# P times V in eight 64x32 array tiles over two PSUM banks: a sliding-window attention block with a gated feed-forward on one Trainium2 core

## The chip, the cores and the metric

The kernel runs on one core of one Trainium2 chip. The metric is device time in microseconds for one execution; the profiled execution is one such run with the hardware profiler on.

## What is computed

x is 2048 x 640. Its normalised form feeds two branches, whose sum is added to x: an attention of 32 heads of 20 dimensions with a causal window of 256, and a gated feed-forward (640 to 1728 and back).

```python
mask = (idx[:, None] - idx[None, :] >= 0) & (idx[:, None] - idx[None, :] < W)   # W = 256
p = softmax(where(mask, q @ k.T * Dh ** -0.5, -1e9))
o = p @ v                       # per head, 2048 x 20
out = x + (o as 2048 x 640) @ wo + (gelu(xn @ w_gate) * (xn @ w_up)) @ w_down
```

## The kernel before

**Stages.** First the layer norm, its transposes and the first projections (until about 100 us); then the attention (about 100 to 570 us); then the rest of the feed-forward; last the down projections. All order on TensorE, ScalarE, VectorE and GpSimd in the attention is the order of the code in `attention` (from L805): nothing is moved by a scheduler.

**Units and slots.** Attention work comes in 32 units, u = 4g + c: eight groups g of eight, each of four heads, and four chunks c of 512 queries. A chunk c > 0 also sees keys of the chunk ahead; a first chunk (c = 0, every fourth unit) does not. Each unit has 14 slots. `SCORES` (L33) says which of the unit's twelve score pieces are made in which slot. `BURSTS` (L32) puts maxima in slots 0, 4 and 8. After every slot's attention work `pull_fill` adds about 2.4 projection matmuls (f32r, 512 columns), so that TensorE always has something to stream.

**Maxima.** `max_pair` (L503) computes q times k for 32-query strips, in eight array tiles of 64 rows by 32 columns: two heads (row halves, each with a PSUM bank of its own) by four strips. VectorE reduces each bank to row maxima (L527). They belong to units one or two ahead. `max_end` (L541) transposes the negated maxima of the next unit in slot 6 (bank `ps_n`), and ScalarE stores them as extra rows of q (L547), so that the scores come out with the maximum already subtracted.

**Scores.** `exp_piece` (L568) makes one score piece for one head: keys on the 128 partitions, queries along the free axis, then ScalarE's exponential (L584) from PSUM into a P tile, f32. The pieces (`pieces`, L549) are packed into three P tiles per unit, X, Z and Y, of four heads each: a key block kb of 128 keys meets the 384 queries from its own start on, cut to the chunk. GpSimd sets what lies outside the window to zero one slot after a tile's last head (`clear`, L588, with L595 for the diagonal and L598 for the far edge). There are three P buffers.

**P times V.** `av_unit` (L601), in slot 0 of the next unit, multiplies the P tiles with v (21 columns per head, the last of ones for the softmax sum; 32 are loaded). Each head has a column tile of the array, 128 rows by 32 columns at `(0, 32 * j)`; all key blocks accumulate in one bank `ps_o`, 24 matmuls for c > 0, 16 for a first chunk. ScalarE copies the bank to `ob` (L613), and three slots later SyncE stores it (L617, L618).

**The ring.** The banks of the maxima, the scores, the negated maxima and P times V all come from one ring of six PSUM banks, tag `ring` (L482, L498); a matmul that takes a bank waits until its former tenant has been read (VectorE for `ps_m`, ScalarE for `ps_e`, `ps_o`, `ps_n`). Which bank is handed out is decided when the program is built. In slot 0 the order is: two pairs of maxima (four banks), P times V (one), two pairs of maxima (four), one score.

**GpSimd** also makes the low parts of split operands (L259, L643) and sums of x (L740), which fill its free time.

Of the kernel before, what the change touches and what calls it, by code (L numbers as in the profile page):

```python
# [9 lines left out]
F32 = mybir.dt.float32  # L10
F32R = mybir.dt.float32r
BF = mybir.dt.bfloat16
AF = mybir.ActivationFunctionType
OP = mybir.AluOpType
# [5 lines left out]
C = 512  # L20
# [9 lines left out]
QROWS = 64 + SR  # L30
NS = 14
BURSTS = 0, 4, 8  # L32
SCORES = {0: range(0, 1), 2: range(1, 5), 4: range(5, 7), 8: range(7, 9), 10: range(9, 12)}  # L33
RATE = 34.05
V1_AT = "gu", 0, 3
VEARLY = 2
# [34 lines left out]
def block_kernel(ctx, tc, x, wqk, wv, wgu, wdo, wdl, out):  # L71
    nc = tc.nc
# [120 lines left out]
    done = set()  # L193
    now = [None]

    def at(slot, fn, *a):
        acts.setdefault(slot, []).append((fn, a))
# [31 lines left out]
    def defer(n, fn, *a):  # L229
        if now[0] is None:  # L230
            fn(*a)
        else:
            at(now[0] + n, fn, *a)
# [190 lines left out]
    with tc.tile_pool(name="lp", bufs=1, side="right") as lp:  # L424
# [5 lines left out]
        ps = psd.tile([128, C], F32, name="ps_u", tag="dn")  # L430
# [49 lines left out]
    vtiles = dict(enumerate(v0[2]))  # L480
    pf.close()
    psr = pp.enter_context(tc.tile_pool(name="psr", bufs=6, space=PSUM, reuse_waits="tile"))  # L482
    ap = pr.enter_context(tc.tile_pool(name="ap", bufs=2, side="right", reuse_waits="tile"))
# [14 lines left out]
    def bank(name):  # L498
        return psr.tile([128, C], F32, name=name, tag="ring")
# [49 lines left out]
    def pieces(c):  # L549
        b = 4 * c  # L550
        X = [(b, 0, 0, 384)] + ([(b - 2, 384, 0, 128)] if c else [])
        Y = [(b + 1, 0, 128, 384), (b + 3, 384, 384, 128)]
        Z = ([(b - 1, 0, 0, 256)] if c else []) + [(b + 2, 256, 256, 256)]
        return X, Z, Y
# [11 lines left out]
    pts = {}  # L566
# [21 lines left out]
    def clear(u, bi):  # L588
        c = u % NC
        pt = pts[u, bi]  # L590
        for p in pieces(c)[bi]:
            for col, diag in diag_tail(*p, c):
# [4 lines left out]
                else:  # L597
                    nc.gpsimd.affine_select(out=a, in_=a, pattern=[[0, 4], [-1, 128]], compare_op=OP.is_ge,  # L598
                                            fill=0.0, base=-1, channel_multiplier=1)

    def av_unit(u):  # L601
        g, c = divmod(u, NC)
        o, v = bank("ps_o"), vtiles[g]
        todo = [(pts[u, bi], *p) for bi, ps in enumerate(pieces(c)) for p in ps]
        for i, (pt, kb, col, q0, n) in enumerate(todo):
            assert (id(v), kb) in done, (u, kb)
            for j in range(4):
                w0_ = kb * 84 + 21 * j
                nc.tensor.matmul(o[32 * j:32 * j + 32, q0:q0 + n], v[:, w0_:w0_ + 32], pt[:, j, col:col + n],  # L609
                                 start=i == 0, stop=i == len(todo) - 1, skip_group_check=True,  # L610
                                 tile_position=(0, 32 * j))
        ob = ap.tile([128, C], F32, name="ob", tag="ob", bufs=1)
        nc.scalar.activation(ob, o, AF.Copy)  # L613

        def store():
            for j in range(4):
                nc.sync.dma_start(od[c].rearrange("(d h) t -> h d t", h=H)[4 * g + j], ob[32 * j:32 * j + DH, :])  # L617
            nc.sync.dma_start(sd[c][4 * g:4 * g + 4, :], ob[DH::32, :])  # L618

        defer(3, store)  # L620

    def load_gu(f):
        raws = []
# [163 lines left out]
    def pull_max(n, slot):  # L787
        for _ in range(n):
            x = next(stream, None)
            if x is None:  # L790
                return
            max_pair(*x)
            if x[1] == 7:
                at(slot + (MXD if slot >= 0 else 4), max_end, x[0])
# [10 lines left out]
    def attention():  # L805
# [18 lines left out]
        for u in range(NU + 1):  # L824
            for i in range(NS):
# [5 lines left out]
                if i == 0 and u:  # L831
                    av_unit(u - 1)
                    flush()
                    pull_max(2, T)
                for s in SCORES.get(i, ()) if u < NU else ():
                    exp_piece(u, s)
# [502 lines left out]
    for j, f in enumerate(range(NFA, NF - 1)):  # L1339
        end = f + 1 == NF - 1  # L1340
        first, second = {i: [] for i in range(4)}, {i: [] for i in range(4)}
# [91 lines left out]
    for n, (p, k) in enumerate(steps):  # L1433
        i = n % (NQD + 1)
        if i == 0:
            begun.clear()
            ps = {b: psn.tile([128, C], F32, name=f"ps_{b}", tag=f"b{b}") for b in (1, 2, 5, 3, 6, 4, 7, 8)}
# [71 lines left out]
```

## Time and profile before

| | us |
|---|---|
| median of 3 runs | 1046.93 (1046.66 to 1049.24) |
| the profiled execution | 1046.71 |
| its span, first to last instruction | 1045.0 |
| TensorE busy in the span | 1034.0 |
| P times V, matmul records x1408, busy | 84.9 |
| maxima on VectorE (L527), 512 reductions, busy | 227.9 |
| exponentials on ScalarE (L584), busy | 195.6 |
| copies of P times V (L613), 32, busy | 19.1 |

How to read it: a matmul's busy time overlaps that of its neighbours, since matmuls are pipelined, so start-to-start distances are used for what a block takes. A group's row has its busy time and the mean duration in ns, then the idle time of the engine just ahead of it and who ended that. A timeline row has the start, the duration of the merged run, engine, line, operation, `out<-in`, and in brackets the idle time ahead and its releaser. In windows rows the busy figures stand in the order PE, PEld, DVE, ACT, POOL.

### The profile page before, as it was taken

To read this page: it belongs to the slowest core of one execution; us is meant where nothing else is said; L and a number is where in the kernel's file an instruction comes from. 1 tells how busy PE (TensorE), PEld (TensorE's weight loads), DVE (VectorE), ACT (ScalarE), POOL (GpSimd) and SP (SyncE) were. 2 spreads that over 40 slices of the span, in tenths; PEclk is the share of its full clock that TensorE was granted. 3 is DMA by queue.
4 is the path that set the end of the run, shared out by engine and by line. 5 is a ranking of instruction groups with operands and counts; after the bars stand their busy time and mean duration, and the time that the engine had idled before them with its cause. 6 is when DMAs were issued, how large, how long until landed. Compare 5 with 4: busy or idle time off the path is not lost.

```text
span 1045.0 us, 25814 instructions
## 1 busy us (share of the span) xinstructions
PE 1034.0 (99%) x9533; PEld 826.2 (79%) x9533; DVE 717.1 (69%) x2007; ACT 513.6 (49%) x1088; POOL 335.9 (32%) x511
## 2 busy tenths in 40 slices
PE   8999999999999999999999999999999999999998
PEld 8987666666677766666667888888888999999998
DVE  8745656666655556666663678877656888888887
ACT  4444666765665666555656522223324553333332
POOL 5222767766464458464634111110110000000000
PEclk9999999999999999999999999999999999999999
DMA  5552465545332355444322556677217864443342
GB/s 200 189 150 61 136 185 157 174 152 183 98 117 74 106 148 153 129 131 140 103 80 82 191 193 235 220 254 246 100 61 255 272 232 137 136 128 114 124 136 92
DMA packets 105192, 158.76 MB, mean 152 GB/s; under 512 B 15421, under 2 KB 60093, under 8 KB 105065
## 3 DMA queue, kind: packets, MB, share of 16 engines
q1 hardware_dynamic: 102680, 150.95, 45.1%
q10 hardware_dynamic: 2384, 6.16, 1.8%
q8 instruction: 75, 1.23, 0.5%
q14 instruction: 53, 0.43, 0.1%
HBM read 101.78 MB, written 54.92 MB: 150 GB/s over the span
## 4 chain that ended last, share of the span: by engine, by line
PE 89%; DVE 3%; DMA 3%; POOL 2%; SPq 1%; ACT 1%; issue 1%; DVEq 0%; POOLq 0%
PE ps_g L953 21%; PE ps L1220 21%; PE ps_d L110 19%; PE ps_e L582 7%; PE ps_v L110 7%; PE ps_o L609 7%; PE ps_m L523 4%; PE ps_g L110 1%; DMA qs<-qd 1%; SPq L494 1%; PE ps_t L181 1%; DMA qd<-pt 1%; POOL pt L259 1%; PE ps_d L356 1%; POOL wql L643 0%
## 5 line engine op out<-in xcount | busy, mean ns | idle before, releaser
L527 DVE CUSTOM_DVE_ANT_0 junk<-ps_m,mask 128x288 bf16<-128x288 f32 (+2 forms) x512 | 227.9, 445 | 155.0 <-PE ps_m L523 97.2
L584 ACT ACTIVATE P<-ps_e 128x512 f32<-128x512 f32 (+2 forms) x384 | 195.6, 578 | 59.8 <-PE ps_e L582 56.1
L1220 PE MATMUL ps<-wb,at 128*128 128x320 f32 x999 | 155.9, 309 | 0.0
L1220 PEld LDWEIGHTS ps<-wb,at 128*128 128x128 f32 x999 | 148.9, 188 | 0.2
L595 POOL TENSOR_SCALAR_AFFINE_SELECT P<-P 128x512 f32<-128x512 f32 x128 | 84.6, 663 | 139.1 <-ACT P L584 138.1
L582 PE MATMUL ps_e<-qs,ks 124*128 124x128 bf16 (+2 forms) x704 | 107.4, 277 | 0.6 <-DVE mx L527 0.5
L110 PE MATMUL ps_d<-xh,wqh 128*128 128x512 f32 x350 | 104.3, 410 | 0.0
L110 PE MATMUL ps_d<-xl,wqh 128*128 128x512 f32 x350 | 104.3, 409 | 0.0
L110 PE MATMUL ps_d<-xh,wql 128*128 128x512 f32 x350 | 103.9, 409 | 0.0
L1220 PE MATMUL ps<-wt,at 128*128 128x320 f32 x552 | 89.3, 309 | 0.4 <-DVE u L1058 0.4
L582 PEld LDWEIGHTS <-ks 124*128 124x128 bf16 x704 | 50.9, 98 | 46.5 <-issue 29.0
L609 PE MATMUL ps_o<-P,v 128*32 128x384 f32 (+2 forms) x1408 | 84.9, 386 | 0.7 <-POOL P L598 0.7
L1220 PEld LDWEIGHTS ps<-wt,at 128*128 128x128 f32 x552 | 82.9, 188 | 0.9 <-DVE u L1058 0.9
L598 POOL TENSOR_SCALAR_AFFINE_SELECT P<-P 128x512 f32<-128x512 f32 x112 | 70.3, 638 | 33.6 <-ACT P L584 33.6
L1174 ACT ACTIVATE at<-ss 128x512 fp32r<-128x512 f32 x59 | 37.3, 632 | 87.6 <-DVE ss L1058 87.5
L103 POOL TENSOR_TENSOR wql<-wr,wqh 128x640 fp32r<-128x640 f32 x11 | 17.6, 1607 | 174.8 <-PE ps_g L953 149.5
L609 PEld LDWEIGHTS ps_o<-P,v 128*32 128x32 f32 x1408 | 41.0, 109 | 40.5 <-issue 20.4
L110 PEld LDWEIGHTS ps_d<-xh,wql 128*128 128x128 f32 x350 | 63.9, 189 | 11.1 <-issue 0.4
L110 PEld LDWEIGHTS ps_d<-xl,wqh 128*128 128x128 f32 x350 | 63.8, 189 | 10.4 <-issue 0.2
L110 PEld LDWEIGHTS ps_d<-xh,wqh 128*128 128x128 f32 x350 | 63.5, 189 | 10.7 <-issue 0.2
L259 POOL TENSOR_TENSOR pt<-r,pt 128x512 bf16<-128x512 f32 x40 | 46.8, 1169 | 63.2 <-ACT pt L258 63.0
L613 ACT ACTIVATE ob<-ps_o 128x512 f32<-128x512 f32 x32 | 19.1, 598 | 86.3 <-PE ps_o L609 76.1
(194 smaller groups left out, 1846.8 us busy)
## 6 DMA issues: line engine op xcount, KB each, us to landing
hr<-hd SPq DMA_DIRECT2D x104, 128.0 KB
hd<-he SPq DMA_DIRECT2D x50, 256.0 KB
wr<-wgu SPq DMA_DIRECT2D x27, 320.0 KB
qs<-qd SPq DMA_DIRECT2D x64, 120.0 KB
ks<-kd SPq DMA_DIRECT2D x64, 120.0 KB
xi<-x SPq DMA_DIRECT2D x16, 320.0 KB
qs<-qd SPq DMA_DIRECT2D x64, 80.0 KB
ks<-kd SPq DMA_DIRECT2D x64, 80.0 KB
```

The source lines that it names most:

```text
L110: nc.tensor.matmul(ps, a(k), b(k), start=n == 0, stop=n == 3 * nk - 1)
L259: nc.gpsimd.tensor_tensor(out=pt[:, l, :], in0=r, in1=pt[:, 1, :], op=OP.subtract)
L523: nc.tensor.matmul(ps[32 * h:32 * h + 32, lo:hi], q[rows, j, q0:q0 + 32], keys, start=True, stop=True, tile_position=(64 * r, 32 * h))
L527: nc.vector.tensor_tensor_reduce(out=junk[:, 0:n], in0=ps[:, 0:n], in1=mask[:, 288 - n:288], scale=1.0, scalar=NEG, op0=OP.add, op1=OP.max ...
L582: nc.tensor.matmul(ps[:, col:col + n], k[0:QROWS, j, kc:kc + 128], q[0:QROWS, j, q0:q0 + n], start=True, stop=True)
L584: nc.scalar.activation(pt[:, j, lo:hi], ps[:, lo:hi], AF.Exp, scale=SCALE)
L595: nc.gpsimd.affine_select(out=a, in_=a, pattern=[[0, 4], [1, 128]], compare_op=OP.is_ge, fill=0.0, base=0, channel_multiplier=-1)
L598: nc.gpsimd.affine_select(out=a, in_=a, pattern=[[0, 4], [-1, 128]], compare_op=OP.is_ge, fill=0.0, base=-1, channel_multiplier=1)
L609: nc.tensor.matmul(o[32 * j:32 * j + 32, q0:q0 + n], v[:, w0_:w0_ + 32], pt[:, j, col:col + n], start=i == 0, stop=i == len(todo) - 1, ski ...
L953: nc.tensor.matmul(ps, i, j, start=first and n == 0, stop=n == len(work) - 1, skip_group_check=True)
L1174: nc.scalar.activation(hi[:, 3:7], s, AF.Copy)
L1220: nc.tensor.matmul(ps[bank][:, 0:HD], *work[bank][j], start=bank not in begun, stop=final[p, bank] == n and j == len(work[bank]) - 1, skip ...
```

## The change

P times V runs in eight array tiles of 64 rows by 32 columns: each key block is cut into two halves of 64 keys, a half for each row half of the array, and each half accumulates in a bank of its own. A half of 64 keys meets only 320 queries, not 384; `windows` works out the columns and pairs a half of one block with a half of the same or another, so that two halves run together. ScalarE copies the two banks, the first to `ob`, the second into the third P tile, which has been read by then; GpSimd adds them one slot later, and the store goes one slot later still. `SCORES` has no score in slot 0 any more, three in slot 2 and two in slot 6, where the negated maxima are.

```diff
-SCORES = {0: range(0, 1), 2: range(1, 5), 4: range(5, 7), 8: range(7, 9), 10: range(9, 12)}
+SCORES = {2: range(0, 3), 4: range(3, 5), 6: range(5, 7), 8: range(7, 9), 10: range(9, 12)}
...
+    def windows(c):
+        r = {}
+        for bi, ps in enumerate(pieces(c)):
+            for kb, col, q0, n in ps:
+                for h in range(2):
+                    first = 128 * (kb - 4 * c) + 64 * h
+                    lo = max(0, first) if kb else 0
+                    hi = min(C, first + 320)
+                    r[h, kb - 4 * c] = bi, kb, col + lo - q0, lo, hi - lo
+        pairs = [(0, 0), (-2, -2), (2, -1), (-1, 2), (1, 1), (3, 3)] if c else [(d, d) for d in range(4)]
+        return [[(h, *r[h, d]) for h, d in enumerate(p)] for p in pairs]
+
     def av_unit(u):
         g, c = divmod(u, NC)
-        o, v = bank("ps_o"), vtiles[g]
-        todo = [(pts[u, bi], *p) for bi, ps in enumerate(pieces(c)) for p in ps]
-        for i, (pt, kb, col, q0, n) in enumerate(todo):
-            assert (id(v), kb) in done, (u, kb)
+        halves, v = [bank("ps_o") for _ in range(2)], vtiles[g]
+        todo = windows(c)
+        for i, pair in enumerate(todo):
             for j in range(4):
-                w0_ = kb * 84 + 21 * j
-                nc.tensor.matmul(o[32 * j:32 * j + 32, q0:q0 + n], v[:, w0_:w0_ + 32], pt[:, j, col:col + n],
-                                 start=i == 0, stop=i == len(todo) - 1, skip_group_check=True,
-                                 tile_position=(0, 32 * j))
-        ob = ap.tile([128, C], F32, name="ob", tag="ob", bufs=1)
-        nc.scalar.activation(ob, o, AF.Copy)
+                for h, bi, kb, col, q0, n in pair:
+                    assert (id(v), kb) in done, (u, kb)
+                    rows, w0_ = slice(64 * h, 64 * h + 64), kb * 84 + 21 * j
+                    nc.tensor.matmul(halves[h][32 * j:32 * j + 32, q0:q0 + n], v[rows, w0_:w0_ + 32],
+                                     pts[u, bi][rows, j, col:col + n], start=i == 0, stop=i == len(todo) - 1,
+                                     skip_group_check=True, tile_position=(64 * h, 32 * j))
+        ob, other = ap.tile([128, C], F32, name="ob", tag="ob", bufs=1), pts[u, 2][:, 0, :]
+        nc.scalar.activation(ob, halves[0], AF.Copy)
+        nc.scalar.activation(other, halves[1], AF.Copy)
+        defer(1, lambda: nc.gpsimd.tensor_tensor(out=ob, in0=ob, in1=other, op=OP.add))
...
-        defer(3, store)
+        defer(4, store)
```

On TensorE, around one P times V of a unit with c > 0, the order before (`ps_m` are maxima, `ps_o` is P times V, its inputs a P tile and v):

```order
L523 MATMUL ps_m<-ks_170,qs_168 32x256
L609 MATMUL ps_o<-P,v 32x384 x4
L609 MATMUL ps_o<-P,v 32x128 x4
L609 MATMUL ps_o<-P,v 32x256 x8
L609 MATMUL ps_o<-P,v 32x384 x4
L609 MATMUL ps_o<-P,v 32x128 x4
L523 LDWEIGHTS qs_168
```

And now, in unit 7, with the engines that a matmul waits for (`Activation` is ScalarE, `Pool` GpSimd, `DVE` VectorE):

```order
L523 MATMUL ps_m<-ks_170,qs_166 32x256
L622 MATMUL ps_o<-P,v 32x320 [waits Activation_49,Pool_49]
L622 MATMUL ps_o<-P,v 32x320 [waits DVE_49]
L622 MATMUL ps_o<-P,v 32x320 x6
L622 MATMUL ps_o<-P,v 32x64 [waits Pool_49]
L622 MATMUL ps_o<-P,v 32x128
```

Eight matmuls stand where four stood, each shorter, and the second, which is the first of the upper half, waits for the second bank. In units 0, 4, 7, 10, 11, 20, 25, 26 and 27 that wait is for VectorE, in the others for ScalarE.

On ScalarE, where one copy and the first scores stood before:

```order
L258 ACTIVATE pt<-r 128x512
L613 ACTIVATE ob<-ps_o 128x512
L584 ACTIVATE P<-ps_e 128x512 x7
L656 ACTIVATE gs<-ps_d 128x512
L657 ACTIVATE he<-ps_d 128x512
```

there are now two copies, and at the same place of the program:

```order
L258 ACTIVATE pt<-r 128x512
L626 ACTIVATE ob<-ps_o 128x512
L627 ACTIVATE P<-ps_o 128x512
L584 ACTIVATE P<-ps_e 128x512 x5
L671 ACTIVATE gs<-ps_d 128x512
L672 ACTIVATE he<-ps_d 128x512
```

The second copy writes into a P tile; seven exponentials ahead of the next other work have become five, the two others standing behind the negated maxima.

## The prediction

> **What bounds the kernel now.** I read the page's busy times first, then its chain, then TensorE's waits in the attention stage, then the timelines around one P times V.
>
> ```profile
> span 1045.0 us, 25814 instructions
> PE 1034.0 (99%) x9533; PEld 826.2 (79%) x9533; DVE 717.1 (69%) x2007; ACT 513.6 (49%) x1088; POOL 335.9 (32%) x511
> PE 89%; DVE 3%; DMA 3%; POOL 2%; SPq 1%; ACT 1%; issue 1%; DVEq 0%; POOLq 0%
> ```
>
> TensorE is busy for 99% of the span and is 89% of the chain that ended last. Its waits within 100 to 570 us, where the attention runs, are these:
>
> ```profile
> PE ps_m L523 <- DMA qs<-qd: 1.5, 3, 0.7
> PE ps_m L523 <- ACT ob L613: 0.7, 2, 0.4
> PE ps_o L609 <- POOL P L598: 0.7, 2, 0.5
> PE ps_e L582 <- DVE mx L527: 0.5, 2, 0.3
> ```
>
> So 3.4 us of waiting in 470 us: a microsecond taken from TensorE's stream comes off the time, unless the shorter stream runs into a wait that it does not meet now. Both sides have to be counted, unit by unit.
>
> **P times V itself.** The TensorE timeline of unit 15 (a unit with a predecessor chunk, 24 of the 32 are such):
>
> ```profile
> 329.47 0.45 PE L523 MATMUL ps_m<-ks,qs 60*32 60x32 bf16 x32
> 329.86 2.80 PE L609 MATMUL ps_o<-P,v 128*32 128x384 f32 x48
> 332.58 0.44 PE L523 MATMUL ps_m<-ks,qs 60*32 60x288 bf16 x16
> 332.95 0.34 PE L582 MATMUL ps_e<-qs,ks 124*128 124x384 bf16 x1
> ```
>
> 24 matmuls leave 48 records: each f32 matmul is two passes. Start to start the block takes 332.58 - 329.86 = 2.72 us. The weight loads show the rhythm of the passes:
>
> ```profile
> 330.20 0.13 PEld L609 LDWEIGHTS ps_o<-P,v 128*32 128x32 f32 x4 [0.19 <-POOL P L598]
> 330.53 1.21 PEld L609 LDWEIGHTS ps_o<-P,v 128*32 128x32 f32 x28 [0.19 <-issue]
> 331.93 0.13 PEld L609 LDWEIGHTS ps_o<-P,v 128*32 128x32 f32 x4 [0.19 <-issue]
> 332.25 0.13 PEld L609 LDWEIGHTS ps_o<-P,v 128*32 128x32 f32 x4 [0.19 <-issue]
> ```
>
> Four loads start together each time, one per head, so the four column tiles run side by side. From 330.53 to 331.93 stand seven passes (two of 128 columns, four of 256, one of 384: 1664 columns) in 1.40 us, 0.841 ns a column. One head's 1536 columns, twice, are 2.58 us; 0.14 us of the 2.72 is start and drain. The same rate gives the short block of unit 16 (first chunk, four pieces, 2 x 1152 columns, 1.94 + 0.14 = 2.08):
>
> ```profile
> 344.32 2.15 PE L609 MATMUL ps_o<-P,v 128*32 128x384 f32 x32
> 346.40 0.44 PE L523 MATMUL ps_m<-ks,qs 60*32 60x288 bf16 x16
> ```
>
> **What the change makes of the block.** A half of 64 keys meets at most 320 queries instead of 384. The eight tiles stand in pairs, and a pair lasts as long as its longer half: 320+128+256+192+320+128 = 1344 columns, twice, 2.26 us; first chunk 384+320+256+128 = 1088, 1.83 us. Add 0.02 for the start. If the halves drift freely the bound is each half's own sum, 1280 (2.15 us); if nothing of the shorter windows is gained, 2.58. I take the pairs.
>
> That eight tiles of 64 rows run side by side is shown by the maxima, which already use that shape: in the row at 332.58 sixteen matmuls of 288 columns in bf16 take 0.37 us. One bf16 column is half an f32 one, 0.42 ns, so two rounds of eight are 0.24 us; sixteen in turn would be 1.9 us. For f32 no row shows it; the other end is a rival below.
>
> The 0.13 to 0.15 us that is left, both in that row and ahead of P times V (329.47 to 329.86: 2 x 288 columns are 0.24 of 0.39), is time in which nothing streams, at each passage between tile shapes. After the change the block has the maxima's shape on both sides. I take 0.11 us as gone at each side; nothing gone is the lower bound. The Trainium skill, TensorEngine Tiling (Array Packing), Key Properties, says that "Changing tiling mode (not just tile) drains the TensorE"; the 0.13 to 0.15 us here agree. By that rule both drains go; if the cost were one of a change of data type, neither would, and my sum would give 3 us less.
>
> TensorE's own saving is then 2.72 - 2.28 + 0.22 = 0.66 us in a normal unit and 2.08 - 1.85 + 0.22 = 0.45 us in a first chunk: 24 x 0.66 + 8 x 0.45 = 19 us. Most of it will not arrive, because of the next three terms.
>
> **First term against it: the ring of six banks and VectorE.** Slot 0 takes four banks for maxima, one for P times V, four more for maxima, and a score; afterwards four, two, four. So the last of the eight maxima takes the bank of the fourth of this same slot, and cannot start until VectorE has reduced that one. Before, it took the third's.
>
> ```profile
> 329.87 0.46 DVE L527 CUSTOM_DVE_ANT_0 junk<-ps_m,mask 128x288 bf16<-128x288 f32 x1 [2.53 <-PE ps_m L523]
> 330.48 0.46 DVE L527 CUSTOM_DVE_ANT_0 junk<-ps_m,mask 128x288 bf16<-128x288 f32 x1
> ...
> 331.70 0.46 DVE L527 CUSTOM_DVE_ANT_0 junk<-ps_m,mask 128x288 bf16<-128x288 f32 x1
> 332.08 0.08 DVE L527 DVE_READ_ACCUMULATOR2_ANT mx<- 128x1 f32 x1
> 332.96 0.46 DVE L527 CUSTOM_DVE_ANT_0 junk<-ps_m,mask 128x288 bf16<-128x288 f32 x1 [0.80 <-PE ps_m L523]
> ```
>
> Counted from the first maximum (329.47), VectorE frees the first bank at 0.86, the second at 1.47, the fourth at 2.69; with 0.05 to wake TensorE (from the copy's end at 243.34 to the row at 243.39, below), 2.74. TensorE is ready for the last pair at 0.39 - 0.11 + 2.28 + 0.13 = 2.69 in a normal unit, 2.26 in a first chunk. Before, the last pair started at 0.39 + 2.72 + 0.13 = 3.24, and 2.60 in a first chunk, with VectorE long done. Hence a normal unit gains 3.24 - 2.74 = **0.50 us**, and a first chunk **loses 0.14 us**. The drains and the free drift now hardly matter in these units: VectorE ends the slot.
>
> The order with its waits shows more: in nine units (0, 4, 7, 10, 11, 20, 25, 26, 27) the second bank of P times V is the bank of this slot's *first* maximum, so the block's second matmul waits until 0.91 instead of starting at 0.28. The block ends 0.6 us later: six normal units gain nothing (0.91 + 2.28 + 0.13 = 3.32 against 3.24), the three first chunks lose 0.1 to 0.3.
>
> In two units the last pair waits now for the bank that P times V itself has just filled:
>
> ```profile
> 137.07 0.31 PE L523 MATMUL ps_m<-ks,qs 60*32 60x288 bf16 x7 [0.37 <-ACT ob L613]
> ...
> 242.61 0.42 PE L523 MATMUL ps_m<-ks,qs 60*32 60x288 bf16 x9
> 243.39 0.31 PE L523 MATMUL ps_m<-ks,qs 60*32 60x288 bf16 x7 [0.37 <-ACT ob L613]
> ...
> 242.74 0.60 ACT L613 ACTIVATE ob<-ps_o 128x512 f32<-128x512 f32 x1 [1.36 <-PE ps_o L609]
> ```
>
> Units 2 and 9 lose that wait: in the new order these pairs take maxima's banks. Unit 9's first maximum stands at 239.50, so its last pair starts 3.89 us on; afterwards VectorE, which had other work first (fourth bank free at 242.91), allows 3.46: 0.4 gained. Unit 2 gains 0.9, with some waiting for GpSimd taken off. Two more kinds of unit differ:
>
> ```profile
> 314.60 0.38 PE L523 MATMUL ps_m<-ks,qs 60*32 60x32 bf16 x28
> ...
> 316.40 0.42 DVE L527 CUSTOM_DVE_ANT_0 junk<-ps_m,mask 128x256 bf16<-128x256 f32 x1
> ...
> 179.85 0.69 DVE L273 TENSOR_TENSOR r<-ps_d,pt 128x512 f32<-128x512 f32 x1 [1.53 <-ACT pt L277]
> ...
> 182.28 0.46 DVE L527 CUSTOM_DVE_ANT_0 junk<-ps_m,mask 128x288 bf16<-128x288 f32 x1
> ```
>
> In units 6, 14, 18 and 22 (here 14) the first four maxima are those of a first chunk and shorter, VectorE is done 2.2 us after the first, and TensorE's 0.31 - 0.11 + 2.28 + 0.13 = 2.61 decides against 3.16 before: 0.55 each, a little less in unit 22. In unit 5 VectorE begins with other work and frees the fourth bank 182.74 - 179.48 = 3.26 us after the first maximum: no gain there.
>
> Sum: nine plain normal units x 0.50 = 4.5; units 6, 14, 18 and 22, 2.1; units 30 and 31, with no maxima around the block, 2 x 0.44 = 0.9; units 2 and 9, 1.3; unit 5, -0.1; the six normal units of the nine, -0.1; first chunks, five x -0.14 and three together -0.7, -1.4. That is **7.2 us**.
>
> **Second term: GpSimd.** It gets one add of 128x512 per unit, which also waits for ScalarE's second copy.
>
> ```profile
> L740 POOL TENSOR_TENSOR tx<-tx,xl 128x256 f32<-128x256 f32 x48 | 35.6, 742 | 1.7
> L103 POOL TENSOR_TENSOR wql<-wr,wqh 128x640 fp32r<-128x640 f32 x11 | 17.6, 1607 | 174.8 <-PE ps_g L953 149.5
> 329.96 0.63 POOL L595 TENSOR_SCALAR_AFFINE_SELECT P<-P 128x512 f32<-128x512 f32 x1
> 336.02 0.63 POOL L595 TENSOR_SCALAR_AFFINE_SELECT P<-P 128x512 f32<-128x512 f32 x1 [3.92 <-ACT P L584]
> ```
>
> Between 742 ns for 256 columns and 1607 for 640 I take 1.3 us. It stands ahead of the clears of the next P tiles. In unit 15 it falls into an idle time of 3.92 us. The last clear of that unit ends at 330.59, 0.73 us after the block has started, and the new block first needs it some 1.9 us after that start: over 1 us to spare. But some units are full:
>
> ```profile
> 179.90:194.90 15.00, 15.00 (x203) 9.76 (x195) 9.71 (x37) 9.63 (x19) 14.30 (x23) 1.00 0.57 171
> sum 462.60, PE 458.82 PEld 306.17 DVE 277.34 ACT 288.79 POOL 273.04; mean PE 14.80 PEld 9.88 DVE 8.95 ACT 9.32 POOL 8.81
> ```
>
> Here GpSimd (the fifth figure after the length) has 0.70 us free, where the mean unit has 6.1. In about three such units the add makes the last clear late by up to 0.5 us: 1.2 us in all, from 0 to 4.
>
> **Third term: ScalarE and DMA.** The second copy costs ScalarE what the first does:
>
> ```profile
> 332.72 0.60 ACT L613 ACTIVATE ob<-ps_o 128x512 f32<-128x512 f32 x1 [2.66 <-PE ps_o L609]
> ```
>
> Both copies end 0.14 + 1.2 = 1.34 us after the block. The scores of slot 2, which take those two banks, come after the last pair (0.13), its drain and two slots of projection work (1.1 us), at about 1.4 us, and the second bank goes to the third of them. It fits, and the score no longer in slot 0 gives ScalarE its 0.6 back there. Slot 6 now has two exponentials behind the negated maxima; slot 8's scores need their banks some 2 us later, where ScalarE takes 0.3 + 1.2. I put 0.5 us on collisions, and 0.5 us on the early waits for qs (the 1.5 us above), which a shorter stream reaches sooner. The store moves one slot behind the add; SyncE's next loads are five slots on.
>
> **Sum.** 7.2 - 1.2 - 0.5 - 0.5 = 5.0 us off. The profiled execution took 1046.71 us (span 1045.0), 0.2 under the runs' median of 1046.93, so I go from there: **1041.7 us**.
>
> **The rivals.**
> - *Waits eat it all* (25%): the margins above are a tenth or two of a microsecond. If ScalarE's second copy comes 0.16 us after the score that wants its bank, in each of 32 units, 5 us are gone: 1046.7; range 1043.8 to 1050. For it: banks are handed out by a rule that does not see times. Against: 38% of ScalarE's time in these units is free (288.79 busy of 462.60). The Trainium skill, same page, PSUM Bottleneck, warns that tiling "speeds up TensorE but not PSUM evacuation"; VectorE's 2.74 against TensorE's 2.69 agrees, and is in my sum.
> - *GpSimd ends the unit* (slower, 9%): should the add push every unit's last clear by its 1.3 us and the time blocked behind the copies, a normal unit waits about 0.25 us at the last pieces, and a first chunk, which now reads the third tile second, 0.9 us: 13 us, less 5, so 1055. It decides once GpSimd has under 1.3 us free between the copies and the last score. For it: the 14.30 above, and that TensorE does wait for it once now (0.53 us before the row at 465.87). Against: mean 8.81 of 14.9.
>
> ```profile
> 465.87 1.07 PE L609 MATMUL ps_o<-P,v 128*32 128x384 f32 x16 [0.53 <-POOL P L598]
> ```
> - *The halves do not run side by side in f32* (4%): a column tile then streams both halves, 2560 columns twice, 4.3 us instead of 2.72: with first chunks at 3.3 instead of 2.08, about 24 x 1.4 + 8 x 1.2, so 1090.
>
> **How the numbers follow.** The forecast with its own range of 1036 to 1043.8 has 60%; waits that eat it 25%; GpSimd 9%; no concurrency 4%; 2% for still faster. A measurement tells about 0.3%, 3.1 us, from no change: faster 0.61, same 0.26, slower 0.13. The range, 1036 to 1049, leaves out the slow rivals.
>
> **What would show it.** P times V start to start near 2.28 us and 1.85, with eight loads together; the last pair of slot 0 at 2.74 us after the first, ended by VectorE; in the nine units the block's second matmul 0.6 us late; no gain in first chunks; GpSimd's add near 1.3 us. It is wrong if TensorE waits often in slots 2 to 10, or for the clears in most units.

## The result, and the profile after

The changed kernel took 1049.09 us (median of 20 executions, 1046.69 to 1051.65) against 1046.42 us of the kernel before (20 executions beside it, 1045.02 to 1049.24): the ratio is 1.0027, 95% interval 1.0019 to 1.0034. It is slower by about 2.7 us, where 5.0 us off was forecast. Its profiled execution took 1047.65 us, with a span of 1045.9, one of the shorter ones: the two profiles differ by 0.9 us, less than the medians do.

Span, busy times and the chain that ended last, from the page after:

```profile
span 1045.9 us, 28723 instructions
PE 1028.8 (98%) x10941; PEld 853.0 (82%) x10941; DVE 726.2 (69%) x2007; ACT 527.7 (50%) x1120; POOL 378.1 (36%) x543
PE 87%; DVE 4%; DMA 3%; POOL 2%; SPq 1%; issue 1%; ACT 1%; DVEq 0%; POOLq 0%; ACTq 0%
```

TensorE has 5.2 us less to do than before (1028.8 against 1034.0), and the span is 0.9 us longer: about 6 us have become idle time (17.1 us of it against 11.0). TensorE's waits within 100 to 570 us say where part of it stands:

```profile
PE ps_m L523 <- DVE mx L527: 2.0, 6, 0.3
PE ps_m L523 <- DMA qs<-qd: 1.8, 3, 0.6
PE ps_o L622 <- DVE mx L527: 1.6, 1, 1.6
PE ps_o L622 <- POOL P L598: 1.3, 1, 1.3
```

Two single waits stand out, of 1.6 and 1.3 us, both in a P times V. The average unit has neither. Unit 15 after, on TensorE:

```profile
328.55 0.45 PE L523 MATMUL ps_m<-ks,qs 60*32 60x32 bf16 x32
328.82 2.42 PE L622 MATMUL ps_o<-P,v 64*32 64x320 f32 x90
...
331.08 0.53 PE L523 MATMUL ps_m<-ks,qs 60*32 60x288 bf16 x13
331.54 0.85 PE L110 MATMUL ps_v<-wvh,xh 128*128 128x320 f32 x4
```

From the first maximum to the projection behind the last one it is 331.54 - 328.55 = 2.99 us; before it was 332.95 - 329.47 = 3.48. That is the 0.49 us of the forecast. So the loss is elsewhere, and a table of how far the changed kernel is behind the kernel before at the first maximum ahead of one unit's P times V (after minus before, in us) finds it. The last four columns are experiments, told below:

```
at unit         after  table only  block only  no add  VectorE adds, store 6
 1              +1.28     +0.83       +0.70     +1.18     +1.39
 4              -0.79     -0.01       -0.69     -0.69     -0.74
20              -2.89     -0.17        0.00     -3.24     -1.80
21              +1.36     +0.56       +2.67     -2.15     -1.12
31              +0.15     -0.21       +3.17     -4.09     -3.37
end of span     +0.93     -0.14       +4.39     -3.22     -3.39
```

At unit 20 the changed kernel was 2.9 us ahead. One unit later it was 1.4 us behind: 4.25 us went in a single unit. (Without the addition it is 1.09 us there, from -3.24 to -2.15.)

Some names for the rows that follow: a projection's result goes to memory in three bf16 parts, pt. VectorE makes the rest r behind the first part (L273), GpSimd makes the last part from r (L259), and r has one buffer, so the next L273 waits for this L259. SyncE stores pt to qd and kd in memory, from which qs and ks, the operands of the maxima and scores, are loaded. tx, with two buffers, are the tiles of GpSimd's sums of x, and td is where SyncE stores them. GpSimd, in that unit:

```profile
391.88 1.27 POOL L628 TENSOR_TENSOR ob<-ob,P 128x512 f32<-128x512 f32 x1
...
395.77 0.45 POOL L658 TENSOR_TENSOR wql<-wr,wqh 128x128 fp32r<-128x128 f32 x1
398.56 0.74 POOL L755 TENSOR_TENSOR tx<-xh,tx 128x256 f32<-128x256 f32 x1 [2.33 <-DMA td<-tx]
...
401.13 1.16 POOL L259 TENSOR_TENSOR pt<-r,pt 128x512 bf16<-128x512 f32 x1
```

SyncE's queue, where the store of the sums starts as the addition ends (391.88 + 1.27 = 393.15), and the stores td stand behind it:

```profile
393.18 1.41 SPq L632 DMA_DIRECT2D od<-ob  x4
394.63 0.49 SPq L633 DMA_DIRECT2D sd<-ob  x1
395.17 2.41 SPq L759 DMA_DIRECT2D td<-tx  x2
```

VectorE, whose rest of a projection waits for GpSimd's L259 and has the maxima behind it, and TensorE, whose second P times V bank is the first maximum's in this unit:

```profile
402.31 0.69 DVE L273 TENSOR_TENSOR r<-ps_d,pt 128x512 f32<-128x512 f32 x1 [3.71 <-POOL pt L259]
```
```profile
400.85 0.45 PE L523 MATMUL ps_m<-ks,qs 60*32 60x32 bf16 x32
401.13 0.70 PE L622 MATMUL ps_o<-P,v 64*32 64x320 f32 x2
403.44 3.42 PE L622 MATMUL ps_o<-P,v 64*32 64x384 f32 x55 [1.61 <-DVE mx L527]
```

And the stretches around it (length, then each engine's busy time, the clock behind POOL's count):

```profile
400.80:403.50 2.70, 1.09 (x42) 0.45 (x47) 1.06 (x3) 0.46 (x1) 2.70 (x5) 1.00 0.09 25
403.50:407.00 3.50, 3.50 (x75) 2.70 (x78) 1.40 (x6) 0.17 (x1) 3.42 (x5) 0.51 0.77 218
407.00:409.00 2.00, 2.00 (x28) 1.23 (x12) 1.40 (x6) 1.63 (x4) 1.82 (x4) 1.00 0.70 201
```

Read them from below: GpSimd is late, VectorE stands 3.71 us, TensorE 1.61 us, and then TensorE's granted clock is half for the next 3.41 us (403.53 to 406.95 in the trace's clock records), which costs another 1.7 (half of it, by estimate, since TensorE is busy throughout: 3.50 of 3.50). The kernel before has no stretch at half clock inside its attention, in its profiled execution. 1.61 + 1.71 = 3.3 of the 4.25 us.

### The profile page after: what moved, and what is told of

It reads as the page before. It is cut to its first block, busy times and chain, and to the rows that moved or that the text cites. A ratio compares the mean times of both kernels' runs of the same rounds, so it can differ in the third digit from the quotient of the medians.

```text
span 1045.9 us, 28723 instructions
## 1 busy us (share of the span) xinstructions
PE 1028.8 (98%) x10941; PEld 853.0 (82%) x10941; DVE 726.2 (69%) x2007; ACT 527.7 (50%) x1120; POOL 378.1 (36%) x543
## 4 chain that ended last, share of the span: by engine, by line
PE 87%; DVE 4%; DMA 3%; POOL 2%; SPq 1%; issue 1%; ACT 1%; DVEq 0%; POOLq 0%; ACTq 0%
PE ps_g L968 21%; PE ps L1235 21%; PE ps_d L110 20%; PE ps_e L582 7%; PE ps_v L110 7%; PE ps_o L622 5%; PE ps_m L523 4%; DVE junk L527 1%; PE ps_g L110 1%; DMA qs<-qd 1%; DMA ks<-kd 1%; PE ps_t L181 1%; SPq L494 1%; POOL pt L259 1%; PE ps_d L356 1%
## 5 line engine op out<-in xcount | busy, mean ns | idle before, releaser
L584 ACT ACTIVATE P<-ps_e 128x512 f32<-128x512 f32 (+2 forms) x384 | 195.4, 573 | 59.4 <-PE ps_e L582 57.9
L622 PE MATMUL ps_o<-P,v 64*32 64x320 f32 (+5 forms) x2816 | 84.4, 353 | 3.0 <-DVE mx L527 1.6
L622 PEld LDWEIGHTS ps_o<-P,v 64*32 64x32 f32 x2816 | 66.6, 107 | 15.0 <-DVE mx L527 6.1
L523 PE MATMUL ps_m<-ks,qs 60*32 60x96 bf16 (+5 forms) x3008 | 64.6, 244 | 4.1 <-DVE mx L527 2.0
L259 POOL TENSOR_TENSOR pt<-r,pt 128x512 bf16<-128x512 f32 x40 | 46.8, 1170 | 54.6 <-ACT pt L258 54.5
```

What stands on the lines that cost most here:

```text
L259: nc.gpsimd.tensor_tensor(out=pt[:, l, :], in0=r, in1=pt[:, 1, :], op=OP.subtract)
L523: nc.tensor.matmul(ps[32 * h:32 * h + 32, lo:hi], q[rows, j, q0:q0 + 32], keys, start=True, stop=True, tile_position=(64 * r, 32 * h))
L584: nc.scalar.activation(pt[:, j, lo:hi], ps[:, lo:hi], AF.Exp, scale=SCALE)
L622: nc.tensor.matmul(halves[h][32 * j:32 * j + 32, q0:q0 + n], v[rows, w0_:w0_ + 32], pts[u, bi][rows, j, col:col + n], start=i == 0, stop=i ...
```

## The experiments

From here the theory was: the block gains what was forecast, and GpSimd's addition, with what is queued behind it, takes it back. Against it stood that the new table of scores is the loss, and that the block itself gains nothing. All times are medians, all ratios are to the kernel before on the same chip.

**One half of the change at a time.** The table alone, in the kernel before:

```diff
-SCORES = {0: range(0, 1), 2: range(1, 5), 4: range(5, 7), 8: range(7, 9), 10: range(9, 12)}
+SCORES = {2: range(0, 3), 4: range(3, 5), 6: range(5, 7), 8: range(7, 9), 10: range(9, 12)}
```

> The kernel before with the new table of scores alone; P times V stays as it was, in one bank. Theory A (the block of P times V gains about 0.5 us in a normal unit, and the changed kernel loses outside it): the table costs the 1.4 us that the changed kernel had lost at unit 0, where scores of slot 8 wait for banks of the same slot's maxima, and little else: 1047.5 to 1048.5 us. Rival B (the table is the whole loss, since the block alone would have brought the 5 us forecast): 1052 us or more. Rival C (the table is free, all of the loss is in the block and its sums): 1046.0 to 1046.8 us.

Measured: 1046.15 us, ratio 1.0007 (0.9998 to 1.0015). The table is free, as rival C had it; theory A's 1.4 us for it was wrong. The 1.25 us that it loses at unit 0 come back by unit 4 (-0.01), so my 1.4 us for unit 0 was a delay, not a loss. The reverse edit, the block with the old table:

> The changed kernel with the table of scores of the kernel before. The score of slot 0 now takes the bank that the first copy of the sums frees, some 0.4 us late in each of 31 units. Theory A: the unit 0 loss of 1.4 us is gone, but the late score eats most of the block's 0.5 us: 1046 to 1052 us. Rival B (the table is the loss): 1040 to 1043 us. Rival C (the block and its sums lose by themselves): 1049 us, unit 0 included.

Measured: 1051.11 us, 1.0053 (1.0040 to 1.0066), within theory A's range; rival B is out. The score left in slot 0 waits for the bank that ScalarE's copy frees. TensorE in unit 15:

```profile
329.99 0.46 PE L523 MATMUL ps_m<-ks,qs 60*32 60x32 bf16 x32
330.26 2.42 PE L622 MATMUL ps_o<-P,v 64*32 64x320 f32 x90
...
333.47 0.32 PE L582 MATMUL ps_e<-qs,ks 124*128 124x384 bf16 x1 [0.43 <-ACT ob L626]
```

Units 13 to 15 now gain 0.01 to 0.04 us each, where they gained 0.45 to 0.49 with the new table. The block and the table need each other; the table costs nothing and the block earns nothing without it.

**The addition.** Left out, with the second copy kept:

```diff
-        defer(1, lambda: nc.gpsimd.tensor_tensor(out=ob, in0=ob, in1=other, op=OP.add))
```

> The changed kernel without GpSimd's addition of the two halves (it leaves out that addition, so the sums are those of the lower keys alone); the second copy of ScalarE stays. Theory A: what the addition starts in unit 20 (store of the sums late, a store queued behind it late, GpSimd waiting for that, VectorE's rest of a projection behind it, the maxima behind that, 1.6 us of TensorE's wait and 3.4 us at half clock) goes, 4.2 us and some tenths in units 6 and 24: 1044 to 1045 us. Rival C (the block gains nothing): within 0.5 us of the changed kernel, 1048.6 to 1049.6 us.

Measured: 1042.45 us, 0.9970 (0.9959 to 0.9981). Against the changed kernel's 1.0027 the addition costs 0.57%, 6.0 us; by the ends of the two intervals 4.0 to 7.8. That is more than theory A's 1044 to 1045 us had, and rival C is out. GpSimd's and VectorE's rows of unit 20 show both waits gone:

```profile
395.14 0.74 POOL L754 TENSOR_TENSOR tx<-xh,tx 128x256 f32<-128x256 f32 x1 [0.35 <-POOL wql L657]
```
```profile
398.91 0.69 DVE L273 TENSOR_TENSOR r<-ps_d,pt 128x512 f32<-128x512 f32 x1 [0.64 <-POOL pt L259]
```

GpSimd's 2.33 us of waiting for td are gone, VectorE's 3.71 have become 0.64, and no half clock follows in the attention. By the table, the difference between the two profiles is 0.35 us at unit 20, 3.51 at unit 21 and 4.24 at unit 31: three quarters of it arise in unit 20 (0.7 us more in unit 24). The addition also keeps the third P tile in use for longer, but no exponential waits for it: in the changed kernel's trace ScalarE's L584 waits for TensorE's scores alone, 56.8 us against 54.3 before.

The second copy, left out as well:

```diff
-        nc.scalar.activation(other, halves[1], AF.Copy)
```

> The changed kernel without the addition and without ScalarE's second copy (it leaves both out, so the sums are those of the lower keys alone). It sizes the copy against the kernel without the addition alone, 1042.45 us. As the prediction had it (0.5 us in all): 1041.5 to 1042.5 us. Rival F (the copy of about 0.6 us in each unit holds up ScalarE's exponentials and with them a bank): 0.2 us in 31 units or more, 1036 us or less.

Measured: 1042.82 us, 0.9967 (0.9955 to 0.9980). The copy costs nothing that can be measured, to within some 2 us by the two intervals. Last, one addition of 32, the one ahead of unit 20's rest of a projection:

```diff
+        if u != 19:
             defer(1, lambda: nc.gpsimd.tensor_tensor(out=ob, in0=ob, in1=other, op=OP.add))
```

> The changed kernel without one addition of GpSimd's, that of unit 19 (it leaves out that one addition, so one group's sums in one chunk are of the lower keys alone); the other 31 stay. GpSimd is 12.6 of 15 us busy from 390 to 405 us in the changed kernel, and the rest of a projection whose store unit 20's loads read stands behind that addition. Theory G (GpSimd's 1.27 us in a stretch where it has no slack, carried on by its queue to VectorE, SyncE and TensorE, and doubled by 3.4 us at half clock): nearly all of unit 20's 4.2 us come back, 1044.5 to 1046 us. Theory S (small losses everywhere, from SyncE's queue or from VectorE): 1048 to 1049.5 us.

Measured: 1045.06 us, 0.9991 (0.9982 to 0.9999). One addition of 1.27 us is worth 0.36%, 3.8 us (2.1 to 5.4 by the ends of the two intervals), by the medians more than half of what all of them cost; in its profile unit 20 loses 1.71 us in place of 4.25. Theory G held: the price is not the instruction's length, but where on GpSimd's queue it falls. A sign of it stood in the profile before the change. GpSimd from 390 to 405 us, before:

```profile
390.00:405.00 15.00, 14.74 (x203) 9.57 (x199) 10.02 (x37) 8.64 (x19) 13.57 (x22) 1.00 0.46 136
```

13.57 of 15 us, 90%, in a kernel whose page says 32%. But a full stretch is a warning and not a price: the fuller one that the prediction quoted (14.30 of 15 us, 179.90 to 194.90) cost nothing. From 180 to 200 us GpSimd is 19.39 of 20 us busy in the changed kernel, which stands at -0.19, -0.12 and -0.20 at units 5, 6 and 7.

**Is it the queue behind the store?** The store of the sums moved from four slots behind the block to nine, and to six:

```diff
-        defer(4, store)
+        defer(9, store)
```

> The changed kernel with the store of the sums issued nine slots after the block in place of four, so that SyncE never stands waiting for the addition with other stores behind it. Theory A: if the chain through SyncE's queue is what held GpSimd in unit 20, it breaks here, and the time is within 0.7 us of the kernel without the addition, about 1045 us. Rival D (GpSimd's own 1.27 us for the addition is what makes it late, not the queue): it stays within 0.7 us of the changed kernel, about 1049 us.

Measured: 1055.48 us, 1.0094 (1.0077 to 1.0112): neither. Unit 20's loss fell to 1.5 us, but the loads of qs came late. TensorE's waits in that kernel:

```profile
PE ps_m L523 <- DMA qs<-qd: 6.4, 8, 1.3
PE ps_m L523 <- DVE mx L527: 2.2, 7, 0.3
PE ps_m L523 <- DMA qd<-pt: 1.1, 1, 1.1
```

> The changed kernel with the store of the sums issued six slots after the block in place of four, the addition where it was. At nine slots the chain of unit 20 was gone, but loads of the scores' operands came late in units 2, 6 and 10. Theory A2 (SyncE's queue standing behind the late addition is the link that matters): 1043 to 1046 us. Theory A1 or rival D (GpSimd is late whatever the queue does): 1048 to 1050 us. If any later store pushes the loads as at nine slots: over 1050 us.

Measured: 1047.57 us, 1.0016 (1.0003 to 1.0028), 11 executions from 1044.82 to 1051.86, between the two ranges. The interval overlaps the changed kernel's, so this alone is unclear; three executions above 1050 us had a mean clock of 0.998 or less. In the profiled one GpSimd does not wait for td ahead of unit 20 any more, and that unit loses 1.5 us instead of 4.25.

The addition itself two slots later, with the store at six:

```diff
-        defer(1, lambda: nc.gpsimd.tensor_tensor(out=ob, in0=ob, in1=other, op=OP.add))
+        defer(3, lambda: nc.gpsimd.tensor_tensor(out=ob, in0=ob, in1=other, op=OP.add))
...
-        defer(4, store)
+        defer(6, store)
```

> The changed kernel with GpSimd's addition issued three slots after the block in place of one, and the store of the sums six slots after it in place of four. GpSimd then no longer stands waiting for ScalarE's second copy (37.2 us in 20 waits in the changed kernel), and does the same work. Theory A1 (the wait ahead of the addition is what makes GpSimd late): 1042.5 to 1044.5 us. Rival D (GpSimd's own 1.27 us are what makes it late): 1048 to 1050 us.

Measured: 1052.54 us, 1.0057 (1.0045 to 1.0069). Theory A1 fell, and the time went above rival D's range too. The addition now ends at 187.47 + 1.29 = 188.76 us in unit 6, again just ahead of its store, and the whole chain stands in three views. GpSimd, SyncE's queue, TensorE:

```profile
187.47 1.29 POOL L628 TENSOR_TENSOR ob<-ob,P 128x512 f32<-128x512 f32 x1
...
194.87 0.73 POOL L755 TENSOR_TENSOR tx<-xh 128x256 f32<-128x256 f32 x1 [4.39 <-DMA td<-tx]
```
```profile
188.79 1.42 SPq L632 DMA_DIRECT2D od<-ob  x4
190.25 0.54 SPq L633 DMA_DIRECT2D sd<-ob  x1
190.84 0.91 SPq L759 DMA_DIRECT2D td<-tx  x2
```
```profile
196.83 1.04 PE L622 MATMUL ps_o<-P,v 64*32 64x320 f32 x32 [1.04 <-POOL P L598]
200.40 3.19 PE L622 MATMUL ps_o<-P,v 64*32 64x256 f32 x61 [2.52 <-POOL P L595]
```

The store waits for the addition, td waits for the store, GpSimd's next tx waits for td (two buffers), the clears of P stand behind tx, and P times V waits for the clears: 3.6 us, and 6.8 us at half clock. As in unit 20 of the changed kernel, the late store stands in the chain.

To cut that link alone, a third tx buffer, paid for with 320 bytes of a tile that nothing uses:

```diff
-    edge.tile([128, 120], F32, name="edge")
+    edge.tile([128, 40], F32, name="edge")
...
-            live[i] = ap.tile([128, w], F32, name="tx", tag="tx")
+            live[i] = ap.tile([128, w], F32, name="tx", tag="tx", bufs=3)
```

> The changed kernel with three buffers in place of two for the tiles tx of GpSimd's other sums (an unused tile made smaller by the same 320 bytes). Nothing of the block, the addition or the queue changes; only GpSimd no longer waits for a store td that stands behind the store of the sums. Theory A2 (addition late, store of the sums late on SyncE, td behind it, GpSimd's next tx waiting for td, and from there VectorE and TensorE): near the kernel without the addition, 1042.5 to 1045 us. Rival D (GpSimd's own 1.27 us in each unit are too much for it, with or without that wait): 1048 to 1050 us.

> The kernel before with three buffers tx, a control. It has no addition, so no store of the sums that is late, though GpSimd waited for td 3 times, 4.8 us in all. Theory A2: little to gain, 1045 to 1046.5 us. If the third buffer is a gain of its own, as large here as in the changed kernel: 1043 us or less.

Measured: 1048.22 us, 1.0020 (1.0009 to 1.0032), and for the control 1048.43 us, 1.0022 (1.0013 to 1.0031). The edit costs the kernel before 2.2 us by itself, all behind the attention (in its profile it is 0.5 us ahead at unit 31 and 2.4 behind at the end; I did not look for the cause). By the time alone this is rival D's range; beside its control the changed kernel loses nothing more (1.0020 against 1.0022). Its profiled execution still loses 4.3 us in unit 20, with no wait for td left: as I read it, L259 is late by GpSimd's own work, its store to qd is late, and the load that reads qd back is what TensorE waits for.

```profile
409.22 0.17 PE L523 MATMUL ps_m<-ks,qs 60*32 60x32 bf16 x1 [1.67 <-DMA qs<-qd]
410.09 0.45 PE L523 MATMUL ps_m<-ks,qs 60*32 60x32 bf16 x31 [0.70 <-DMA qs<-qd]
```

This execution (1051.36 us, mean clock 0.998) is one of three of its kind. The other nine have a mean clock of 1.0, which none of the changed kernel's 20 has (3.41 us at half clock take 0.0016 off the mean): with the third buffer the half clock is gone in most executions. So A2 looks like part of the loss, and as I had put it is not the whole. Moving the stores td to another queue gained nothing:

```diff
-            defer(4, lambda: nc.sync.dma_start(td[p][i][:, k, half * w:half * w + w], t))
+            defer(4, lambda: nc.scalar.dma_start(td[p][i][:, k, half * w:half * w + w], t))
```

> The changed kernel with the stores td issued from ScalarE's queue in place of SyncE's, so that they no longer stand behind the store of the sums; two buffers as before. Theory A2: 1042.5 to 1046 us, a little over the three buffers since ScalarE now issues 32 stores and may wait for GpSimd in some. Rival D: 1048 to 1050 us.

Measured: 1049.65 us, 1.0030 (1.0019 to 1.0041), in rival D's range. Its profiled execution was the shortest of its ten (span 1044.1, mean clock 1.0, where eight have 0.998 or less), so its profile explains little.

**The addition on VectorE.** It takes one bank directly and ScalarE's copy of the other, and stands behind the second pairs of maxima in slot 0:

```diff
-        ob, other = ap.tile([128, C], F32, name="ob", tag="ob", bufs=1), pts[u, 2][:, 0, :]
+        ob = ap.tile([128, C], F32, name="ob", tag="ob", bufs=1)
...
-        nc.scalar.activation(other, halves[1], AF.Copy)
-        defer(1, lambda: nc.gpsimd.tensor_tensor(out=ob, in0=ob, in1=other, op=OP.add))
+        sums = lambda: nc.vector.tensor_tensor(out=ob, in0=halves[1], in1=ob, op=OP.add)
...
         defer(4, store)
+        return sums
...
-                    av_unit(u - 1)
+                    sums = av_unit(u - 1)
                     flush()
                     pull_max(2, T)
+                    sums()
```

> The changed kernel with the two halves added by VectorE, from the second bank and ScalarE's copy of the first, behind the second pairs of maxima of slot 0; no second copy and no addition on GpSimd. Theory A (the loss is GpSimd's addition and what waits for it): the kernel without the addition ran at 1042.45 us, and VectorE's 0.7 us lie behind the maxima that TensorE waits for, so 1042 to 1044 us. Rival E (VectorE sets the end of slot 0 and of what follows, so that its 0.7 us in each unit come to TensorE as waits for a projection's bank or for slot 2's scores): half of 0.7 us in 31 units, 1052 us or more.

> VectorE's addition (1051.0 us with two buffers) with three buffers tx. In the trace of that kernel GpSimd waited for td 17.2 us in 8 waits, the longest 6.1 us, with no addition of its own; the store of the sums stood on SyncE waiting for VectorE. Theory A2: the same chain with the addition on another engine, so it goes here too: 1042 to 1045 us. Rival E (VectorE's 0.7 us in each unit): 1049 us or more.

Measured: 1051.00 us, 1.0049 (1.0036 to 1.0062), and with three tx buffers 1047.08 us, 1.0007 (0.9999 to 1.0016), of which the control puts 2.2 us on the edit itself. Both times lie between the two ranges. The first looks like rival E, but the profile speaks for the queue: with no addition of its own, GpSimd waited up to 6.08 us for td, since the store stood on SyncE until VectorE's addition (291.13 to 291.82) was done.

```profile
291.85 1.40 SPq L631 DMA_DIRECT2D od<-ob  x4
293.29 0.50 SPq L632 DMA_DIRECT2D sd<-ob  x1
```
```profile
297.57 0.73 POOL L755 TENSOR_TENSOR tx<-xh,tx 128x256 f32<-128x256 f32 x1 [6.08 <-DMA td<-tx]
```

With the same addition and the store at six slots:

```diff
-        defer(4, store)
+        defer(6, store)
```

> VectorE's addition behind the maxima of slot 0, as in the kernel of 1051.0 us, with the store of the sums six slots after the block in place of four, two buffers tx. No addition on GpSimd and no store on SyncE that waits for a late one, so by both links of the theory (GpSimd's own time, SyncE's queue) what is left is VectorE's 0.7 us: 1042 to 1045 us. Rival E (VectorE's own time is dear): 1048 us or more.

Measured: **1044.09 us**, 0.9985 (0.9976 to 0.9993), faster than both kernels, and in the range of the theory. The page and TensorE's waits of that kernel:

```profile
PE 1027.1 (99%) x10941; PEld 852.8 (82%) x10941; DVE 734.4 (71%) x2039; ACT 512.8 (49%) x1088; POOL 335.5 (32%) x511
```
```profile
PE ps_m L523 <- DVE mx L527: 2.5, 8, 0.3
PE ps_e L582 <- DVE mx L527: 1.2, 3, 0.5
PE ps_m L523 <- DMA qs<-qd: 0.6, 1, 0.6
```

No wait of TensorE in these 470 us is over 0.6 us, and none is followed by half clock in the attention. The place on VectorE's queue matters: one slot later, the second bank comes late for slot 2's scores. Beside the lines shown, the edit takes out `return sums` and the call `sums()`:

```diff
-        sums = lambda: nc.vector.tensor_tensor(out=ob, in0=halves[1], in1=ob, op=OP.add)
+        defer(1, lambda: nc.vector.tensor_tensor(out=ob, in0=halves[1], in1=ob, op=OP.add))
```

> As the kernel before it in this list, with VectorE's addition issued in slot 1 in place of behind slot 0's maxima, so that VectorE takes the rest of a projection and ScalarE's copy first. If the place on VectorE's queue is worth anything, it differs by over 1.5 us from it: faster, if the addition had held VectorE waiting for ScalarE's copy, 1041 to 1043 us; slower, if slot 2's scores wait for the second bank, 1045 us or more.

Measured: 1048.88 us, 1.0023 (1.0014 to 1.0032), 4.8 us more, and in TensorE's waits a row that the kernel before it did not have:

```profile
PE ps_e L582 <- DVE ob L627: 2.6, 8, 0.5
```

**Is a later store a gain by itself?** In the kernel before (three slots to six), and in the changed kernel without the addition (four to six):

> The kernel before with the store of the sums six slots after the block in place of three; its sums are ready long before either. Theory (the later store helps only where the sums are late): no gain, 1045.5 to 1048 us, a loss if SyncE's loads are pushed. If the later store is a gain by itself: 1043 us or less, and then the kernel of 1044.1 us owes nothing to the change.

> The changed kernel without the addition (it leaves it out, the sums are those of the lower keys alone) and with the store six slots after the block; with four it was 1042.45 us. Theory (the later store helps only where the sums are late): 1042 to 1044.5 us. If the later store is a gain by itself: 1040 us or less.

Measured: 1045.33 us, 0.9994 (0.9984 to 1.0004), no difference; and 1045.33 us, 0.9988 (0.9978 to 0.9998), where with four slots it was 0.9970. The later store gains nothing by itself. Without an addition it is 2 us dearer by the medians, above the theory's range, though the two intervals overlap. The profiled executions of both kernels show where a later store can cost: in unit 3, around 155 us, TensorE waits 2.03 us (before) and 1.89 us (changed) for loads of qs, and a stretch of 3.41 us at half clock follows. (Two of 11 executions of the one and three of 11 of the other have the mean clock of 0.998 that goes with it.) The later store helps where the sums are late:

```
ratio to before      store 4    store 6
no addition           0.9970     0.9988
GpSimd adds           1.0027     1.0016
VectorE adds          1.0049     0.9985
```

With the store at six, VectorE's addition costs nothing that can be measured (0.9985 against 0.9988), and GpSimd's costs 0.28%, 2.9 us (0.5 to 5.2 by the ends of the intervals). That these 2.9 us are GpSimd's own time is argued, not shown. With the store at four VectorE's addition pays for SyncE's queue as well, which the intervals show; for GpSimd's they overlap.

## Why the prediction was wrong

**Failed: the second term, GpSimd.** "1.2 us in all, from 0 to 4" was 6.0 us (4.0 to 7.8). The length of the addition was right (1.28 us against 1.3), and so was unit 15, where it falls into idle time. Wrong was what I followed behind it. I asked only whether the clears of P come late for P times V, about 0.5 us in three full units. Behind the same instruction stood three more things: L259, for which VectorE's rest of a projection waits, with the maxima behind it, and whose result goes to memory and comes back as the qs of the same stretch; the store on SyncE, with td behind it and GpSimd's own tx behind td; and TensorE's clock. Leaving out the one addition of unit 19 gave 3.8 us back. The prediction quoted a full stretch for GpSimd (14.30 of 15 us, which cost nothing) and named "GpSimd ends the unit" as a rival, but let it decide only when every unit was full; one stretch was enough to turn the sign. How the 6.0 us divide between GpSimd's own 1.27 us in that stretch and the queue behind the late store stays open: the third tx buffer took the half clock away in most executions, the store at six brought 1.1 us that the intervals don't tell from nothing, and neither took all.

**Right: the block and VectorE's bound.** 0.50 us in a normal unit was 0.49 in unit 15. There VectorE frees the fourth bank at 331.16 + 0.08 = 331.24, 2.69 us after the first maximum, as forecast, and the last pair follows at 331.30:

```profile
331.16 0.08 DVE L527 DVE_READ_ACCUMULATOR2_ANT mx<- 128x1 f32 x1
```

Without the addition, eight of the nine plain normal units gain 0.33 to 0.55 us, and none of the nine units with the late second bank gains over 0.2. Of these, unit 7 (TensorE, first maximum to the projection 213.11 - 209.49 = 3.62 us; the block runs 2.87 us from its first weight load to its last, in unit 15 2.25):

```profile
209.49 0.45 PE L523 MATMUL ps_m<-ks,qs 60*32 60x32 bf16 x32
209.77 2.96 PE L622 MATMUL ps_o<-P,v 64*32 64x320 f32 x82
...
213.11 1.19 PE L110 MATMUL ps_d<-xl,wqh 128*128 128x512 f32 x4
```

Halves of 64 keys run side by side in f32, so that rival is out. The sum without the GpSimd term was 7.2 - 0.5 - 0.5 = 6.2 us. The kernel without the addition gives the check: in its profile it is 3.2 us under the kernel before. From unit 0 to unit 31 its position moves from +1.36 to -4.09, which is 5.45 us gained, against 6.2 in the sum; behind the attention it gives back 0.9. Unit 20 alone accounts for as much as is lacking: it loses 1.09 us without the addition too, where 0.1 to 0.3 was forecast. The 19 us that the prediction named as TensorE's own saving count the passage behind the block twice, in 2.72 - 2.28 and in the 0.22 (about 0.11 us in each unit); the 7.2 us do not use them.

**Missing: unit 0 and the tail.** The sum started at unit 0's block and had nothing for the 1.25 to 1.54 us ahead of it (after minus before at unit 0, in the four kernels of the table above that have the new `SCORES`), where slot 8's scores wait for that slot's own maxima, nor for what lies behind the attention. The table alone has the same delay and regains it by unit 4; whether the changed kernel does, the runs don't tell. The 0.9 us behind the attention have no cause shown, and the kernel with VectorE's addition and the store at six gives back nothing there. Of the 7.7 us by which the forecast missed (5.0 off, 2.7 on), 4.8 lie in the GpSimd term and, by the profile without the addition, about 1.4 at unit 0, 0.9 in the tail and 0.7 in the attention.

**ScalarE and DMA**, 0.5 each: the second copy costs nothing measurable. TensorE's waits for qs, 1.5 us before, are 1.8 in the changed kernel and 2.1 without the addition, so that term was about right.

**"Waits eat it all"** came nearest in size (1043.8 to 1050), by another mechanism: not 0.16 us of ScalarE in each unit, but some 4 us in one.

## What to carry to other kernels

Price an added instruction on a "free" engine stretch by stretch, not by the engine's mean share. A full stretch is only where to look (one of 90% cost 3.8 us here, one of 95% nothing): follow everything queued behind the instruction, and the DMA queue that waits for its result, to the bounding engine. Issue a store late enough that its queue never waits for the data, but before the queue's next urgent loads: here nine slots gave 1055.5 us, and with VectorE's addition four and six gave 1051.0 and 1044.1 (with GpSimd's 1049.1 and 1047.6, which the intervals don't tell apart). And give the addition to an engine with a gap at the right moment: on VectorE, 686 ns behind the maxima cost nothing measurable, and one slot later 4.8 us.

## What the runs showed of the hardware

A short idle time can cost TensorE as much again, but need not. In the changed kernel 1.61 us of wait ended at 403.44, and the granted clock was half from 403.53 to 406.95, 3.41 us; with three tx buffers waits of 1.67 and 0.70 us were followed by another 3.41; with the addition two slots later, 1.04 and 2.52 us by 6.83. All 20 executions of the changed kernel have a mean clock of 0.998, five of six without the addition 1.000. The Trainium skill, TensorE: Matmul & The Clock Gate, Part 1, gives a window of about 3.4 us, which the 3.41 here agrees with, and an idle window as the condition; unlike that, 1.61 us without a matmul had been enough here, in a stretch of 2.70 us with 1.09 busy. The length of the wait alone does not decide it: without unit 19's addition TensorE waited 2.04 us for the clears, until 465.09, and with VectorE's addition and the store at four 1.78 us, until 468.63, and neither was followed by half clock. What decides stays open.

The same two-input addition took 1284 ns on GpSimd and 686 ns on VectorE:

```profile
L628 POOL TENSOR_TENSOR ob<-ob,P 128x512 f32<-128x512 f32 x32 | 41.1, 1284 | 40.9 <-ACT P L627 37.2 <-DMA qs<-qd 3.5
```
```profile
L627 DVE TENSOR_TENSOR ob<-ps_o,ob 128x512 f32<-128x512 f32 x32 | 21.9, 686 | 7.0 <-PE ps_d L110 4.6 <-ACT ob L626 2.4
```

The Trainium skill, GPSIMD Engine Reference, 4.1 Engine selection, has such an operation about twice as slow on GpSimd; 1.87 agrees.
